# Load order, sine tables, first taps and x's tails in the opening of a two-branch kernel

## The chip, the cores and the metric

The kernel runs on one core of one Trainium2 chip. Its time is the device time of one launch in microseconds (us). Five instruction streams run side by side and wait for each other through semaphores: TensorE (PE: matrix products into PSUM), VectorE (DVE: elementwise), ScalarE (ACT: activations, and copies out of PSUM), GpSimd (POOL: here mostly constants, and DMAs that add), and SyncE (SP: issues DMAs).

## The reference, cut to what matters

Two unrelated branches share the inputs' shape (2048 rows, 576 columns, bf16); their outputs stand side by side.

```
# branch A: dilated local attention, 32 heads of 18, 8 positions at distance 2
qkv = x @ wqkv
logits[s, w] = q[s] . k[s - 2 w] * 18 ** -0.5       # masked where s - 2 w < 0
o = softmax(logits) @ v[s - 2 w];  a = o @ wo
# branch B: a short convolution, a gate, a long convolution, a gate
k_shift[s] = sum over t < 4 of k[s - t] * shift_k[:, t]
kv = k_shift * v
y = causal convolution of kv with ssm_k over 2048 positions, by FFT   # float32
y = y + kv * ssm_D;   b = q * y
out = concat(a, b)
```

## The kernel before, in words

Branch A projects x by wqkv. PE needs x transposed (columns on partitions): 4 blocks of 128 columns and a tail of 64. The first half of x (rows 0 to 1023) comes in two quarters by plain DMA and is transposed on PE (`transpose_x`, `tail_x`, L450 and L455), then copied from PSUM by ACT and, for two blocks of the first quarter, DVE (L510, L511, L521, L460). The second half comes by transposing DMAs (`turn_x`, L236); its tail comes by plain DMA (L235) and is transposed on PE in `transpose_tail` (L473, evicted by ACT L475). `x5(jj)` holds the tails of half jj: its lower 64 partitions those of one quarter, its upper 64 those of the other.

`project_first(jp, ct0)` (L483, L485, evicted at L487) makes q for 256 columns of quarter jp; four calls do the first half of q. `project` (L363 for the four blocks, L374 for the tails, evicted at L397) appends the rest as small pieces of work, "units", for column tiles ct and halves jj. So the jj = 1 units are the first users of the second half of x.

Branch B works on four blocks of 512 rows. `taps(i)` is DVE work: products of k with the four tap weights `skb` (L560), sums (L564), a product with v (L580). The weights are spread over the partitions by PE and ACT (`spread_taps`, L496, L499). k is held as seven rows per partition, 0 to 6; output row c of tap j reads row j + c, so the newest tap (3) reads rows 3 to 6 and tap 2 rows 2 to 5. Block 0's k is loaded in two pieces, rows 3 to 6 and then rows 0 to 2; partition 0 has a memset on POOL and a small POOL DMA of its own (L190, L191). `mirror` folds a finished block on PE (L589) and ACT (L592). The convolution is done by products with tables of sines: TK for the filter, TX for kv, TI (TX transposed on PE in `table_i`, L438, evicted at L442) for the way back. A table is made of an int32 product and offset on DVE (L421, twice), an AND that takes it modulo the period (L422), and a Sin on ACT (L423). The transforms of the filter are L610, L611 and L670, those of kv L766 and L768.

Each engine's order is written out by hand. Work for PE and ACT is held in `units`; `until()` takes as many from its front, at a given place in the DVE work, as the next number in `PLACES` says. `AT` says where the folds go into `units`, `FKS` and `FXS` how the two kinds of transforms and v's projections are interleaved. DVE work stands in program order: four blocks of taps, logits (L822), softmax, weighted sums (L947), spectral products (L1098). SP issues its DMAs in program order: x's first quarter, wqkv's q part, x's second quarter, k's block 0, the k part, v's block 0, k's block 1, x's second half, v's block 1, and so on. After eight DMAs a semaphore is used again, and the ninth waits for the first to land. POOL makes its constants (`identn` to `identn2`, L247 to L298) in program order, with `zero_pads` (L410, L412) behind them. There are two kinds of PSUM buffers, A and B, two of each, that are handed out in turn.

Of the kernel before, what the change touches and what calls it, by code (L numbers as in the profile page):

```python
# [12 lines left out]
ALU = mybir.AluOpType  # L13
FP32 = mybir.dt.float32
BF16 = mybir.dt.bfloat16
I32 = mybir.dt.int32
PSUM = bass.MemoryType.PSUM

PLACES = (
    15, 4, 11, 2, 1, 0, 3, 4, 6, 4, 13, 4, 4, 0, 4, 3, 4, 2, 1, 3, 4, 3, 5, 5, 0, 7, 2, 2, 2, 1, 2, 2, 2, 2, 3,  # L20
    1, 0, 3, 2, 0, 8, 3, 0, 1, 12, 1, 1, 0,
)

FKS = (
    3, 1, 0, 0, 0, 0, 0, 0, 0, 0, 0, 0, 0, 0, 0, 0, 0, 0, 1, 0, 0, 0, 0, 2, 0, 0, 2, 0, 0, 0,
)
FXS = (
    7, 2, 0, 12, 13, 2, 0, 0, 4,
)
# [5 lines left out]
AT = (  # L35
    2, 10, 17,
)
# [8 lines left out]
def kernel(  # L46
# [89 lines left out]
    def load_w(eng, comp, to=None):  # L136
        low, high = (to[:, 0:4, :], to[:, 4, :]) if to is not None else \
            (view(xw, w_at(0, comp), [[D, 4], [1, D]]), wq(4, comp, 0, D))
        eng.dma_start(low, A_wqkv[0:512, comp * D:(comp + 1) * D].rearrange("(kb p) a -> p kb a", p=128))
        for r in range(2):  # L140
            eng.dma_start(high[64 * r:64 * r + 64, :], A_wqkv[512:576, comp * D:(comp + 1) * D])

# [40 lines left out]
    def load_k(i):  # L183
# [5 lines left out]
        if i == 0:  # L189
            nc.gpsimd.memset(kj[0:1, 0:3, :], 0.0)  # L190
            nc.gpsimd.dma_start(kj[0:1, 3:7, :], kf[0:4, :].unsqueeze(0))  # L191
            low = [(1, 49), (49, 64)]
        for a, b in ((3, 7), (0, 3)) if i == 0 else ((0, 7),):
            for p0, p1 in low:
                eng.dma_start(kj[2 * p0:2 * p1:2, a:b], bass.AP(
                    tensor=kf.tensor, offset=kf.offset + (r0 + 4 * p0 - 3 + a) * D,
                    ap=[[4 * D, p1 - p0], [D, b - a], [1, D]]))
# [31 lines left out]
    load_w(nc.sync, 0)  # L229
    load_x(1)  # L230

    def turn_x(h):

        r0 = 1024 + 512 * h
        nc.sync.dma_start(xnat[:, 2 + h, :, 512:576], xf[r0:r0 + 512, 512:576].rearrange("(sb p) c -> p sb c", p=128))  # L235
        nc.sync.dma_start_transpose(view(xw, 6 * HB + 512 * h, [[1024, 4], [1, 512]]), xf[r0:r0 + 512, 0:512])  # L236

# [59 lines left out]
    nc.gpsimd.tensor_scalar(ident2[:], ident[:], 2.0, None, op0=ALU.mult)  # L297
    nc.gpsimd.tensor_scalar(identn2[:], ident[:], -2.0, None, op0=ALU.mult)  # L298

    qk = main.tile([128, 4 * S + 1024 + 4 * KW + KWH], BF16, name="qk")  # L300
# [114 lines left out]
    zero_pads(1)  # L415
    nc.vector.tensor_copy(rp[:], rp_i[:])
    nc.vector.tensor_scalar(rp[64:128, 4:8], rp[64:128, 4:8], -510.0, None, op0=ALU.add)

    def table(n_i, T, vec, cols, period, offs):
        for n in range(2):  # L420
            nc.vector.tensor_scalar(n_i[:, n, :], vec, rp[:, cols[n]:cols[n] + 1], offs[n], op0=ALU.mult, op1=ALU.add)  # L421
        nc.vector.tensor_single_scalar(n_i, n_i, period - 1, ALU.bitwise_and)  # L422
        return lambda: nc.scalar.activation(T, n_i, ACT.Sin, bias=pib[:], scale=-2.0 * np.pi / period)  # L423

# [39 lines left out]

    def early(f, us):
        f()
        clk["P"] += us

    def transpose_tail(jj):
        pt = pp.tile([128, 512], FP32, name="ps_x", tag="B")  # L470
        for jp in range(2):
            for sb in range(4):
                nc.tensor.matmul(pt[64 * jp:64 * jp + 64, 128 * sb:128 * sb + 128], xnat[:, 2 * jj + jp, sb, 512:576],  # L473
                                 ident[:], start=True, stop=True, tile_position=(0, 64 * jp))
        nc.scalar.activation(x5(jj), pt[:], ACT.Copy)  # L475

    def project_first(jp, ct0):
# [25 lines left out]
    spread_taps(0)  # L503
    sines = [table_k(0), table_k(1)]
    pts = [pair_x() for _ in range(2)]
# [7 lines left out]
    spread_taps(256)  # L513
    sines += [table_x(0), table_x(1)]
    project_first(0, 0)
    pts = [pair_x() for _ in range(2)]
    for n in range(2):
# [4 lines left out]
    copy_tail(1, pts[0])  # L522
    project_first(0, 2)
    sines[2]()
    for n in range(2):
        project_first(1, 2 * n)
        sines[3 - 3 * n]()
    for jj in range(2):
        if jj:
            project(0, jj)  # L530
        project(1, jj)
        if jj == 0:
            units.append((0.43, partial(early, partial(transpose_tail, 1), 0.43), "x"))
    project(0, 2)
    project(1, 2)

    def with_sine(f, n):
        f()
        sines[n]()
        if n == 1:  # L540
            nc.gpsimd.memset(TK[0:1, 0, 1, :], 0.5)
            for gi, sg in enumerate((1, -1, -1, 1)):
                nc.gpsimd.memset(TK[0:1, 0, 0, 128 * gi:128 * gi + 128], sg * 0.5)

    for n in range(2):
        units.insert(4 + 4 * n, (0.85, partial(early, partial(table_i, n), 0.85), "x"))
    for n, u in zip((1,), (1,)):
        units[n] = units[n][:1] + (partial(with_sine, units[n][1], u),) + units[n][2:]
# [5 lines left out]
    def taps(i):  # L554
# [12 lines left out]
        if i == 0:  # L567
            mult(view(kv, 0, [[4 * D, 1], [D, 4], [1, D]]), 3, 1)
            mult(view(tB, 0, [[4 * D, 1], [D, 4], [1, D]]), 2, 1)
            add(pair[0])  # L570
# [733 lines left out]
```

## Time and profile before

| what | value |
|---|---|
| runs (three) | 213.08, 213.27, 213.81 us; median 213.27 |
| profiled execution, span from first to last instruction | 211.5 us |
| the profiled execution's own time | not listed; its span is 1.8 us below the median |
| busy: PE, DVE, ACT, POOL | 200.9, 197.3, 151.0, 69.3 us |
| granted TensorE clock, mean | 0.998 |
| DMA, moved over the span | 36.12 MB, mean 171 GB/s |

In the timeline a row has start, length, engine, line, operation, result and operands, and in brackets the idle time of that engine before it and what ended it; rows in a run are merged (x8). In the groups by line a row has the count, the busy total and the mean of one in ns. In the chain of work that ended last a row has start, length and what ran; it gives a PE instruction only the time until the next could go, so its lengths are a bit shorter than those of the timeline. "DMA to landing" counts from the issue. L numbers are lines of the kernel before.

### The profile page before, as it was taken

Reading aid. Unit: us, or ns where it says so; the run is one execution under the profiler, and the core shown is the slowest. Engines: PE = TensorE matmul, PEld = TensorE weight load, DVE = VectorE, ACT = ScalarE, POOL = GpSimd, SP = SyncE. Lnnn points to the kernel's source line nnn. Section 1 sums busy time; section 2 is a strip of 40 time slices with the busy share of each in tenths; the row PEclk is TensorE's granted clock in tenths of the full one; section 3 lists DMA queues with packets and bytes.
Section 4 is the critical chain, followed back from the end, with each engine's and each line's share of the span. In section 5 each row is a group of like instructions: output and inputs, shape, how many; then the busy total and the mean of one; then the engine's idle time right before and its main releaser. Section 6 shows DMA issues by size and latency. Waiting matters only on the chain.

```text
span 211.5 us, 5096 instructions
## 1 busy us (share of the span) xinstructions
PE 200.9 (95%) x2122; PEld 112.5 (53%) x2122; DVE 197.3 (93%) x150; ACT 151.0 (71%) x218; POOL 69.3 (33%) x104
## 2 busy tenths in 40 slices
PE   7999899999879999999999999999999999999891
PEld 2543344445545556563345566765567667676560
DVE  7989999999978999979979999999999999899982
ACT  3799766967797989984378688864487896765640
POOL 8999991023391367220090000004240000202000
PEclk9999999999999999999999999999999999999999
DMA  6999999999092636998999896589993105453034
GB/s 204 297 317 239 248 323 322 183 238 286 8 135 33 87 56 105 187 159 187 226 222 228 141 232 154 103 211 249 209 278 107 60 3 160 123 167 115 3 106 117
DMA packets 34084, 36.12 MB, mean 171 GB/s; under 512 B 17459, under 2 KB 28847, under 8 KB 34062
## 3 DMA queue, kind: packets, MB, share of 16 engines
q1 hardware_dynamic: 26380, 23.11, 43.8%
q0 software_dynamic: 5216, 10.19, 24.8%
q10 hardware_dynamic: 2466, 2.51, 3.6%
q8 instruction: 16, 0.26, 0.5%
q14 instruction: 6, 0.05, 0.1%
HBM read 13.11 MB, written 4.72 MB: 84 GB/s over the span
## 4 chain that ended last, share of the span: by engine, by line
PE 78%; ACT 10%; issue 3%; SPq 2%; DVE 2%; DMA 2%; DVEq 0%; ACTq 0%
PE ps_proj L363 13%; PE ps_z L1126 9%; PE ps_wo L1020 8%; PE ps_acc L964 7%; PE ps_inv L1158 7%; PE ps_fx L766 7%; PE ps_log L837 4%; PE ps_proj L483 4%; PE ps_fk L610 3%; ACT Ks L670 3%; PE ps_proj L374 2%; DMA Ks<-Ks 2%; SPq L212 2%; PE ps_rev L650 1%; PE ps_sk L496 1%
## 5 line engine op out<-in xcount | busy, mean ns | idle before, releaser
L363 PE MATMUL ps_proj<-xw 128*128 128x512 bf16 x160 | 37.5, 380 | 0.5 <-ACT qk L397 0.5
L822 DVE TENSOR_TENSOR av<-qk 128x4096 bf16<-128x4096 bf16 (+1 forms) x16 | 31.5, 2017 | 1.9 <-ACT xw L592 1.9
L363 PEld LDWEIGHTS <-xw 128*128 128x128 bf16 x160 | 14.4, 98 | 20.1 <-issue 4.8
L1139 ACT ACTIVATE av<-ps_z 128x768 bf16<-128x768 f32 x23 | 17.5, 811 | 5.6 <-PE ps_z L1126 5.6
L768 ACT ACTIVATE xw<-ps_fx 128x576 bf16<-128x576 f32 x32 | 18.8, 673 | 2.4 <-PE ps_fx L766 2.4
L397 ACT ACTIVATE qk<-ps_proj 128x1024 bf16<-128x1024 f32 x14 | 14.3, 1025 | 8.3 <-PE ps_proj L374 4.7
L670 ACT ACTIVATE Ks<-ps_fk 128x576 bf16<-128x576 f32 x32 | 19.0, 688 | 1.1 <-PE ps_fk L611 1.0
L1098 DVE TENSOR_TENSOR qk<-xw,Ks 128x2304 bf16<-128x2304 bf16 x14 | 18.6, 1355 | 1.0 <-PE ps_z L1126 0.7
L560 DVE TENSOR_TENSOR tB<-kj,skb 128x4608 bf16<-128x4608 bf16 (+1 forms) x8 | 19.3, 2416 | 0.1
L766 PE MATMUL ps_fx<-xw,TB 128*128 128x288 bf16 x128 | 17.9, 286 | 0.8 <-ACT xw L592 0.7
L1020 PE MATMUL ps_wo<-qk 128*128 128x288 bf16 x128 | 17.9, 287 | 0.0
L610 PE MATMUL ps_fk<-Ks,TB 128*128 128x384 bf16 x62 | 16.4, 326 | 1.2 <-ACT Ks L670 0.9
L1158 PE MATMUL ps_inv<-av,TI 128*128 128x288 bf16 (+1 forms) x112 | 15.6, 292 | 0.6 <-ACT av L1139 0.6
L766 PEld LDWEIGHTS <-TB 128*128 128x128 bf16 x128 | 12.0, 98 | 6.7 <-issue 3.5
L964 PE MATMUL ps_acc<-av,ident 64*64 64x512 bf16 x160 | 15.3, 379 | 0.0
L611 PE MATMUL ps_fk<-Ks,TB 128*128 128x192 bf16 x62 | 15.2, 246 | 0.0
L1087 POOL DMA_DIRECT2D TB<-in_B_q_dram x4 | 3.0, 738 | 36.7 <-DVE v L1098 23.5
L397 ACT ACTIVATE v<-ps_proj 128x1024 bf16<-128x1024 f32 x9 | 9.3, 1043 | 7.8 <-PE ps_proj L363 4.3
L1020 PEld LDWEIGHTS <-qk 128*128 128x128 bf16 x128 | 11.5, 98 | 6.2 <-issue 3.6
L968 ACT ACTIVATE qk<-ps_acc 128x1024 bf16<-128x1024 f32 x8 | 8.2, 1025 | 8.3 <-PE ps_acc L964 8.3
L947 DVE TENSOR_TENSOR av<-Ks,v 128x4096 bf16<-128x4096 bf16 x6 | 13.6, 2285 | 0.1
L1158 PEld LDWEIGHTS <-TI 128*128 128x128 bf16 x112 | 10.5, 98 | 5.6 <-issue 2.7
(194 smaller groups left out, 465.7 us busy)
## 6 DMA issues: line engine op xcount, KB each, us to landing
Ks<-Ks POOLq DMA_DIRECT2D x7, 576.0 KB, 8.3
TB<-av SPq DMA_DIRECT2D x12, 256.0 KB, 4.9
kj<-in_B_k_dram SPq DMA_DIRECT2D x6, 504.0 KB, 6.1
vt<-in_B_v_dram SPq DMA_DIRECT2D x8, 288.0 KB, 5.0
Ks<-av SPq DMA_DIRECT2D x8, 256.0 KB, 6.0
out_dram<-qk ACTq DMA_DIRECT2D x5, 288.0 KB, 3.2
Ks<-in_A_x_dram SPq DMA_DIRECT2D x2, 576.0 KB, 5.2
xw<-in_A_wqkv_dram SPq DMA_DIRECT2D x2, 576.0 KB, 6.0
```

The costliest lines, as they stand in the source:

```text
L363: nc.tensor.matmul(ps[:, jp, :], wq(kb, comp, 128 * ct, 128), xT(kb, 1024 * jj + 512 * jp, 512), **se)
L397: nc.scalar.activation(view(t, o + pad + 1024 * jj, [[512, 2], [1, 512]]), ps[:], ACT.Copy)
L560: dve(2304 * n, lambda: nc.vector.tensor_tensor(to, view(kj, row * D, [[D, n], [D, 4], [1, D]]), view(skb, row * D, [[D, n], [0, 4], [1, D ...
L610: nc.tensor.matmul(o[:, 0:2], w, rhs[:, 0:2], start=start, stop=stop)
L670: nc.scalar.activation(view(Ks, k_at(m, cs ^ (m & 1)) + 96 * gi, [[768, 3], [384, 2], [1, 96]]), acc3(ps), ACT.Copy, scale=(PSG, MSG)[cs][ ...
L766: nc.tensor.matmul(ps[:, pm, 0:HD], TX[:, 2 * pm + c, 128 * gi:128 * gi + 128], kv[:, 2 * c + pm, HD * h:HD * h + HD], start=(c == 0), sto ...
L768: nc.scalar.activation(view(xw, HB * XG[i] + 96 * gi + 1152 * h, [[HB, 2], [384, 3], [1, 96]]), view(ps, 0, [[512, 2], [96, 3], [1, 96]]), ...
L822: return P, at, step, dve(1024 * nj, lambda: nc.vector.tensor_tensor(view(P, at, [[step, 4], [256, nj], [1, 256]]), view(t, o + 256 * hh, ...
L964: nc.tensor.matmul(acc[64 * o:64 * o + 64, h, :], ident[64 * h:64 * h + 64, 64 * h:64 * h + 64], view(P, 256 * u, [[2048, 2], [1, 256]])[6 ...
L1020: nc.tensor.matmul(ps[:, r, 0:HD], oT(hh, j + 2 * r, t)[:, o:o + 128], wo[:, t // 2, t % 2, HD * h:HD * h + HD], start=(t == 0 and h == 0) ...
L1126: nc.tensor.matmul(view(acc[r], 512 * h, [[192, 2], [96, 2], [1, 96]])[o:o + 64], w[64 * h:64 * h + 64, 64 * h:64 * h + 64], pr[64 * h:64 ...
L1158: nc.tensor.matmul(ps[:, c, 0:n], TI[:, sl, pm, 128 * c:128 * c + 128], Yall[:, j % 2, pm, sl, c0:c0 + n], start=(pm == 0 and sl == 0), st ...
```

## The change

It has five parts and new schedule numbers.

- Loads: block 0's k rows 3 to 6 are issued ahead of x's second quarter, in two DMAs that include partition 0 (the POOL DMA L191 goes); rows 0 to 2 follow it. The 64 tail rows of each weight load go to both halves of the partitions by one DMA in place of two.
- Tables: the factors are scaled so that the period is 65536. The low 16 bits of the int32 product, read as a signed 16-bit number, are the phase, so the AND goes. TX is made first, ahead of TK; its sines run on ACT right after the third spread of the weights, and TI is made from it around the transposes of x's second quarter. TK's sines are attached to the second and fourth unit. TK's second half is multiplied out on DVE inside the taps of block 0.
- Taps of block 0: the product of row 2 is split into outputs 1 to 3, which need rows 3 to 5 alone, and output 0.
- Tails of x's second half: the first transposing DMA takes five blocks (the fifth holds the 64 tail columns, and 64 columns more that are overwritten); for the second quarter of that half a transposing DMA of the last 128 columns goes to `xend`, and a POOL DMA moves its upper 64 partitions into `x5(1)`. `transpose_tail` goes.
- Order: two `project_first` calls stand ahead of the second quarter's transposes, and the schedule numbers differ.

```
 PLACES = (
-    15, 4, 11, 2, 1, 0, 3, 4, 6, 4, 13, 4, 4, 0, 4, 3, 4, 2, 1, 3, 4, 3, 5, 5, 0, 7, 2, 2, 2, 1, 2, 2, 2, 2, 3,
-    1, 0, 3, 2, 0, 8, 3, 0, 1, 12, 1, 1, 0,
+    5, 15, 9, 3, 0, 1, 3, 4, 6, 8, 10, 3, 4, 0, 4, 3, 3, 3, 1, 4, 3, 3, 5, 5, 0, 7, 2, 2, 2, 1, 2, 2, 2, 2, 3,
+    1, 0, 3, 2, 1, 14, 3, 0, 1, 18, 1, 1, 0,
...
-    3, 1, 0, 0, 0, 0, 0, 0, 0, 0, 0, 0, 0, 0, 0, 0, 0, 0, 1, 0, 0, 0, 0, 2, 0, 0, 2, 0, 0, 0,
+    3, 0, 0, 1, 0, 0, 0, 0, 0, 0, 0, 2, 0, 0, 0, 0, 1, 0, 0, 0, 0, 0, 0, 0, 0, 0, 2, 0, 0, 0,
...
-    7, 2, 0, 12, 13, 2, 0, 0, 4,
+    7, 15, 3, 5, 5, 2, 0, 0, 4,
...
 AT = (
-    2, 10, 17,
+    0, 7, 20,
...
-        for r in range(2):
-            eng.dma_start(high[64 * r:64 * r + 64, :], A_wqkv[512:576, comp * D:(comp + 1) * D])
+        eng.dma_start(high, A_wqkv[512:576, comp * D:(comp + 1) * D].unsqueeze(0).to_broadcast([2, 64, D]))
...
             nc.gpsimd.memset(kj[0:1, 0:3, :], 0.0)
-            nc.gpsimd.dma_start(kj[0:1, 3:7, :], kf[0:4, :].unsqueeze(0))
-            low = [(1, 49), (49, 64)]
         for a, b in ((3, 7), (0, 3)) if i == 0 else ((0, 7),):
-            for p0, p1 in low:
+            if (i, a) == (0, 0):
+                load_x(1)
+            for p0, p1 in low if i or a else ((1, 49), (49, 64)):
...
     load_w(nc.sync, 0)
-    load_x(1)
...
-        r0 = 1024 + 512 * h
-        nc.sync.dma_start(xnat[:, 2 + h, :, 512:576], xf[r0:r0 + 512, 512:576].rearrange("(sb p) c -> p sb c", p=128))
-        nc.sync.dma_start_transpose(view(xw, 6 * HB + 512 * h, [[1024, 4], [1, 512]]), xf[r0:r0 + 512, 0:512])
+        def turn(to, n, c0):
+            nc.sync.dma_start_transpose(to, bass.AP(tensor=xf.tensor, offset=xf.offset + (1024 + 512 * h) * D + c0,
+                                                    ap=[[D, 512], [1, 128 * n]]))
+        if h == 0:
+            turn(view(xw, 6 * HB, [[1024, 5], [1, 512]]), 5, 0)
+            return
+        turn(view(xw, 6 * HB + 512, [[1024, 4], [1, 512]]), 4, 0)
+        turn(xend, 1, D - 128)
+    xend = view(Ks, 7 * HB, [[1, 512]])
...
     nc.gpsimd.tensor_scalar(identn2[:], ident[:], -2.0, None, op0=ALU.mult)
+    nc.gpsimd.dma_start(x5(1)[64:128], xend[64:128])
...
-    nc.vector.tensor_copy(rp[:], rp_i[:])
-    nc.vector.tensor_scalar(rp[64:128, 4:8], rp[64:128, 4:8], -510.0, None, op0=ALU.add)
+    nc.vector.tensor_scalar(rp[:, 0:4], rp_i[:, 0:4], 32.0, None, op0=ALU.mult)
+    nc.vector.tensor_scalar(rp[0:64, 4:8], rp_i[0:64, 4:8], 16.0, None, op0=ALU.mult)
+    nc.vector.tensor_scalar(rp[64:128, 4:8], rp_i[64:128, 4:8], -510.0, 16.0, op0=ALU.add, op1=ALU.mult)
...
-            nc.vector.tensor_scalar(n_i[:, n, :], vec, rp[:, cols[n]:cols[n] + 1], offs[n], op0=ALU.mult, op1=ALU.add)
-        nc.vector.tensor_single_scalar(n_i, n_i, period - 1, ALU.bitwise_and)
-        return lambda: nc.scalar.activation(T, n_i, ACT.Sin, bias=pib[:], scale=-2.0 * np.pi / period)
+            nc.vector.tensor_scalar(n_i[:, n, :], vec, rp[:, cols[n]:cols[n] + 1], offs[n] * (65536 // period),
+                                    op0=ALU.mult, op1=ALU.add)
+        low = n_i.rearrange("p n f -> p (n f)").bitcast(I16).rearrange("p (n f w) -> p n f w", n=2, w=2)[:, :, :, 0]
+        return lambda: nc.scalar.activation(T, low, ACT.Sin, scale=2.0 * np.pi / 65536)
...
-    sines = [table_k(0), table_k(1)]
+    sines = [table_x(0), table_x(1)]
...
     spread_taps(256)
-    sines += [table_x(0), table_x(1)]
+    sines.append(table_k(0))
+    sines[0]()
+    sines[1]()
     project_first(0, 0)
+    project_first(0, 2)
+    table_i(0)
...
     copy_tail(1, pts[0])
-    project_first(0, 2)
-    sines[2]()
+    table_i(1)
     for n in range(2):
         project_first(1, 2 * n)
-        sines[3 - 3 * n]()
...
-        if jj == 0:
-            units.append((0.43, partial(early, partial(transpose_tail, 1), 0.43), "x"))
...
-    for n in range(2):
-        units.insert(4 + 4 * n, (0.85, partial(early, partial(table_i, n), 0.85), "x"))
-    for n, u in zip((1,), (1,)):
+    for n, u in zip((1, 3), (2, 3)):
...
-            mult(view(tB, 0, [[4 * D, 1], [D, 4], [1, D]]), 2, 1)
+            for c, n in ((1, 3), (0, 1)):
+                dve(n * D, lambda: nc.vector.tensor_tensor(
+                    pair[0][:, c:c + n], kj[:, 2 + c:2 + c + n], skb[:, 2:3, :].to_broadcast([128, n, D]), ALU.mult))
+                if c:
+                    sines.append(table_k(1))
```

More of the change, by code (lines that the diff above doesn't have):

```diff
@@ L16 @@
 I32 = mybir.dt.int32
+I16 = mybir.dt.int16
 PSUM = bass.MemoryType.PSUM
 PLACES = (
-    15, 4, 11, 2, 1, 0, 3, 4, 6, 4, 13, 4, 4, 0, 4, 3, 4, 2, 1, 3, 4, 3, 5, 5, 0, 7, 2, 2, 2, 1, 2, 2, 2, 2, 3,
-    1, 0, 3, 2, 0, 8, 3, 0, 1, 12, 1, 1, 0,
+    5, 15, 9, 3, 0, 1, 3, 4, 6, 8, 10, 3, 4, 0, 4, 3, 3, 3, 1, 4, 3, 3, 5, 5, 0, 7, 2, 2, 2, 1, 2, 2, 2, 2, 3,
+    1, 0, 3, 2, 1, 14, 3, 0, 1, 18, 1, 1, 0,
 )
 FKS = (
-    3, 1, 0, 0, 0, 0, 0, 0, 0, 0, 0, 0, 0, 0, 0, 0, 0, 0, 1, 0, 0, 0, 0, 2, 0, 0, 2, 0, 0, 0,
+    3, 0, 0, 1, 0, 0, 0, 0, 0, 0, 0, 2, 0, 0, 0, 0, 1, 0, 0, 0, 0, 0, 0, 0, 0, 0, 2, 0, 0, 0,
 )
 FXS = (
-    7, 2, 0, 12, 13, 2, 0, 0, 4,
+    7, 15, 3, 5, 5, 2, 0, 0, 4,
 )
@@ L463, in pair_x @@
         return pp.tile([128, 2, 1024], BF16, name="ps_x", tag="B")
[L465 to L475, printed above, removed]
     def project_first(jp, ct0):
@@ L539, in with_sine @@
         sines[n]()
-        if n == 1:
+        if n == 3:
             nc.gpsimd.memset(TK[0:1, 0, 1, :], 0.5)
```

## The prediction

> **What bounds the kernel now.** I read the page's first part, then the busy times by stage, the chain of work that ended last, the waits of VectorE (DVE), and last the instructions in order of time up to 64 us. Engine totals, from the page:
>
> ```profile
> span 211.5 us, 5096 instructions
> PE 200.9 (95%) x2122; PEld 112.5 (53%) x2122; DVE 197.3 (93%) x150; ACT 151.0 (71%) x218; POOL 69.3 (33%) x104
> ```
>
> Two engines are nearly full, so the order in which they wait for each other decides. By stage (columns: stretch, length, then busy us and count for PE, PEld, DVE, ACT, POOL, the granted clock, DMA share, GB/s):
>
> ```profile
> 24.00:53.00 29.00, 29.00 (x202) 12.48 (x203) 28.52 (x17) 20.48 (x28) 11.22 (x23) 1.00 1.02 270
> 53.00:64.00 11.00, 8.85 (x85) 5.56 (x84) 9.18 (x9) 9.48 (x16) 6.96 (x9) 1.00 0.52 74
> 64.00:107.00 43.00, 42.08 (x380) 22.81 (x376) 40.58 (x25) 33.08 (x52) 14.56 (x14) 1.00 0.73 131
> 107.00:180.00 73.00, 72.90 (x910) 44.94 (x902) 71.85 (x49) 53.68 (x79) 11.05 (x15) 1.00 0.71 169
> ```
>
> From 24 to 53 us PE does not stop at all. From 53 to 64 it loses 2.15 us, DVE 1.82 us, and ACT (9.48 of 11) is the fullest. After that PE is full again. Two of DVE's later waits, and rows of the timeline at 64 us with the longest one:
>
> ```profile
> DVE av L882 <- ACT av L879: 1.3, 1, 1.3
> DVE av L947 <- PE ps_log L837: 1.1, 1, 1.1
> ```
>
> ```profile
> 63.34 1.05 PE L837 MATMUL ps_log<-av,E 128*32 128x512 bf16 x16
> 64.06 3.43 DVE L822 TENSOR_TENSOR av<-qk 128x4096 bf16<-128x4096 bf16 x2 [1.85 <-ACT xw L592]
> ```
>
> DVE had three logit products ready and stood 1.85 us, until 64.06, for a buffer that PE's first L837 group (from 63.34) empties. So at 64 us DVE is early and PE late, and the later waits too are for PE or ACT. What the first 53 us do to PE therefore passes to the end; what they do to DVE does not, as long as the DVE wait stays above zero.
>
> **The change: VectorE.** Rows that price it, of the groups, the timeline, and L179's landing times:
>
> ```profile
> L421 DVE TENSOR_SCALAR Ks<-Ks,rp 128x512 int32<-128x512 int32 x8 | 3.6, 494 | 0.0
> L422 DVE TENSOR_SCALAR Ks<-Ks 128x1024 int32<-128x1024 int32 x4 | 2.8, 708 | 0.1
> 11.96 1.36 DVE L560 TENSOR_TENSOR xw<-kj,skb 128x2304 bf16<-128x2304 bf16 x1 [0.82 <-DMA kj<-in_B_k_dram]
> 16.02 2.56 DVE L560 TENSOR_TENSOR tB<-kj,skb 128x4608 bf16<-128x4608 bf16 x1
> 26.75 2.56 DVE L560 TENSOR_TENSOR tB<-kj,skb 128x4608 bf16<-128x4608 bf16 x1
> 3.12 0.59 SPq L179 DMA_DIRECT2D Ks<-in_A_x_dram  x1
> DMA to landing us min/median/max: 4.1/5.2/6.3
> 8.28 1.02 ACT L499 ACTIVATE skb<-ps_sk 128x1024 bf16<-128x1024 f32 x1
> ```
>
> Four ANDs go (2.8 us). Block 0's first product now starts at 11.96, after waiting for k. Moved ahead of x's second quarter, k's first block (equally large) takes that quarter's place: issue 3.12 plus the longer of the two landings of that line, 6.3, is 9.4. The tap weights are out at 8.28 + 1.02 = 9.3. So the product starts near 9.4, 2.56 us earlier. Behind it now stand the last table's two products (3.6 / 8 = 0.45 each, 0.9) and a split product: from 1.36 for 2304 elements and 2.56 for 4608 an instruction's fixed part is 0.16. The three small instructions that replace the cast and the subtraction add one such 0.16 before 9.4, in time that is free. DVE ends block 0 ahead by 2.56 - 0.9 - 0.16 = 1.5 us. This buys nothing: the 1.85 us wait becomes 3.3. If k landed no sooner than now, DVE would be 1.06 late, still inside the 1.85.
>
> **TensorE and ScalarE up to 24 us.** The sines of TX now run before the first projection's eviction, and both inverse tables (L438) surround the transposes of x's second quarter.
>
> ```profile
> 7.79 1.91 PE L483 MATMUL ps_proj<-xw 128*128 128x512 bf16 x8
> 10.17 1.07 PE L450 MATMUL ps_x<-ident,Ks 128*128 128x128 bf16 x16
> 11.51 1.90 PE L483 MATMUL ps_proj<-xw 128*128 128x512 bf16 x8
> 11.62 1.94 ACT L521 ACTIVATE xw<-ps_x 128x1024 bf16<-128x1024 bf16 x2 [0.32 <-PE ps_x L455]
> 23.84 1.08 ACT L442 ACTIVATE TI<-ps_ti 128x512 bf16<-128x512 f32 x2
> 24.00 1.89 PE L363 MATMUL ps_proj<-xw 128*128 128x512 bf16 x8 [0.55 <-ACT qk L397]
> ```
>
> ```profile
> 20.88 1.02 ACT qk L397
> 21.90 1.04 ACT TB L423
> 27.39 0.57 PE ps_ti L438 x16
> 28.93 0.35 PE ps_x L473 x8
> 29.28 1.83 PE ps_proj L363 x8
> ```
>
> The second fence is of the chain of work that ended last. One early projection takes PE 10.17 - 7.79 = 2.38, x's transposes 11.51 - 10.17 = 1.34. PE afterwards: projection to 10.17, second to 12.55, first table to 13.12, transposes to 14.46, second table to 15.03. ACT: free at 9.3, two sines 2 x 1.04 to 11.38, eviction (1.02) to 12.40, so the table's PSUM is free in time; the second eviction can start at 12.6 and ends at 13.6; table eviction 1.08 to 14.7; copies of x 0.97 each, to 15.65 and 16.6. The third projection needs the first copy for its first two matmuls (1.83 / 4 = 0.46) and the second for the next: PE stands 0.6 and then 0.5, together 1.1 us. Gone are the 0.55 wait at 24.00 and the tail transposes (0.35). Sum on PE: 1.1 - 0.55 - 0.35 = **+0.2 us**. From both sides: if ACT's sines did not delay the copies, -0.9; if PE also stood for the table's PSUM as at 24.00, +0.75. I take +0.2, since every term but the waits is a row. x's second quarter lands 2 us later (behind 590 KB more), at 11.4, and is wanted at 13.1: hidden, 1.7 us of cover.
>
> **x's tails by DMA.** PE loses its eight transposes and ACT one copy. SP loses the two tail loads, and one of each pair of weight loads and of k's split loads, about 0.59 us of issue each (the row at 3.12), and gains a fifth block in the first transposing DMA and a third one. POOL loses its k DMA and gains one that moves the second half's tail, and PE's jj = 1 tails wait for it. Behind it on POOL stand memsets for k's pads and TK, and the filter's copies, which wait for their data until 42.2. Behind the transposes on SP stand block 1's v and block 2's k; if these come late, DVE loses some of a lead that buys nothing. Rows of source lines and of the timeline, and a fold from the chain:
>
> ```profile
> L236 SPq DMA_TRANSPOSE xw<-in_A_x_dram x2: 2422/3606/4789, 14.9 to 20.9; - x2
> DMA to landing us min/median/max: 4.8/6.6/8.3
> 3.84 0.87 POOL L191 DMA_DIRECT2D kj<-in_B_k_dram  x1
> 11.61 0.20 POOL L277 TENSOR_SCALAR_AFFINE_SELECT E<-ones 128x32 bf16<-128x32 bf16 x1
> 16.13 2.52 POOL L279 TENSOR_SCALAR_AFFINE_SELECT E<-E 64x32 bf16<-64x32 bf16 x1
> 29.66 1.42 POOL L298 TENSOR_SCALAR identn<-ident 128x128 bf16<-128x128 bf16 x1
> L726 POOL DMA_DIRECT2D Ks<-Ks x3: 538/543/632, 42.2 to 47.7; - x3
> DMA to landing us min/median/max: 2.5/3.4/4.3
> 35.53 0.61 PE ps_fold L589 x8
> ```
>
> When PE wants it: the first jj = 1 matmul is at 29.28 now; plus 0.2, plus a fold (0.61) that the new AT puts ahead of it, 30.1; its tails come 1.83 later, **31.9**. When it lands: the DMA is queued on POOL behind L298, which ends at 31.08 now. A POOL operation that takes 0.20 at 11.61 takes 2.52 beside DVE's product of 16.02 and ends when that ends: one passes per DVE product, eleven between 11.96 and 31.08. In the new order POOL starts 0.87 earlier, and DVE, free of the ANDs, stands from about 7.9 to 9.4, where six selects pass; I estimate 13 left at 9.4, give or take three. The thirteenth DVE instruction from there is block 1's second double product, which ends at 26.75 + 2.56 = 29.3 now and at 27.8 then. The transposes: SP reaches the first about 2 us sooner, near 13; 5/4 of 4.79 brings it to 19, the second (2.4 to 4.8) to 21.4 to 23.8, and the last lands 4.8 later, 26.2 to 28.6. So the POOL DMA starts at about 28 and lands 3.4 later, 31.4: 0.5 us before PE wants it. I count 0. The ends are 0 (26.2 + 2.5 is long before) and 4.3: three more POOL operations pass with three more DVE products of 1.36, to 31.9, and land 4.3 later, at 36.2.
>
> [...]
>
> **Reordered fillers.** Two transforms of x (0.5 us of PE each) and two of the filter (0.49 each) move ahead of the fifth logit group.
>
> ```profile
> 78.52 1.02 ACT L842 ACTIVATE av<-ps_log 128x1024 bf16<-128x1024 f32 x1 [0.18 <-PE ps_log L837]
> 82.87 0.20 DVE L865 TENSOR_TENSOR av<-av,maskb 32x128 bf16<-32x128 bf16 x1
> ```
>
> That eviction ends 2 us later, at 81.5, and its reader starts at 82.87: hidden, 1.3 us of cover. A transform moved behind the L837 group at 106.47 can cut the last DVE wait of 1.1 by 0.5; PE is full there, so I count 0 and keep -0.5 for the range.
>
> **Sum.** +0.2 on a span of 211.5, 211.7. The span is 1.8 below the median of the runs, 213.27, and I carry that over: **213.5 us**.
>
> **Rivals.** *The tail lands late*: POOL passes fewer selects than I estimate and PE stands at its first jj = 1 tails. It decides from a landing after 31.9. One or two products more (1.36 each, less the 0.5) cost 0.9 or 2.2, on average 1.5: 213.5 + 1.5 = 215.0. For it: only 0.5 us of cover on a chain of thirteen steps; against: POOL's head start. *DVE's lead arrives*: the folds are done sooner, and PE's and ACT's idle time at 53 to 64 us (2.15 and 1.52) shrinks by the lead, 213.27 - 1.5 = 211.8. For it: DVE is 93% busy and has hardly a wait from 64 to 180; against: at 53 to 64 it waits for PE, and the last fold's operand was already there. It decides if the 1.85 us wait shrinks rather than grows. *No change from loading k first*: the start at 9.4 fails because ACT's weights or k come late; by the 1.06 above that ends in 213.5 too.
>
> **How the numbers follow.** About 0.3% (0.64 us) is what a measurement of this kernel can tell from no change. Likeliest case 0.44, its own range 212.6 to 214.2 (-0.9 and +0.75 about zero): same 0.35, slower 0.06, faster 0.03. Late tail 0.30: slower. Lead arrives 0.26: faster 0.25, same 0.01. Together faster 0.28, same 0.36, slower 0.36. The range, 211.6 to 215.8, takes in both rivals' values; beyond it, with some 0.15, lie the last 2 us of the late tail and reorderings that add to the lead.
>
> **What would show it.** Right: block 0's first product near 9.4; the first L822 after the negations waiting over 3 us; PE standing about 1.1 us around 15 to 17; no PE wait on a POOL DMA near 32; first L837 near 63.5. Wrong: PE standing at L374 near 32, a first L837 before 62.9, or the third projection starting without a wait.

## The result, and the profile after

The changed kernel takes **219.34 us** in the median of six runs (216.76 to 220.75), the kernel before 213.32 beside it (212.92 to 214.28): the ratio is **1.025, 95% interval 1.020 to 1.029**. The forecast was 213.5 with a range of 211.6 to 215.8, so it missed, by 5.8 us. The six times of the changed kernel lie 4.0 us apart, those of before 1.4. That scatter is the kernel's own, as will be seen; the ratios and intervals leave out executions more than 1.5% above the fastest of a kernel, so I give the extremes too.

The execution shown took 220.37 us, 1.7 above its span. The page's first part, and the busy times by stage (columns as in the prediction):

```profile
span 218.7 us, 5070 instructions
PE 203.1 (93%) x2114; PEld 112.6 (51%) x2114; DVE 195.2 (89%) x148; ACT 150.1 (69%) x217; POOL 55.6 (25%) x104
```

```profile
24.00:53.00 29.00, 25.78 (x125) 9.82 (x124) 26.54 (x15) 16.66 (x21) 3.62 (x11) 0.88 1.04 262
53.00:64.00 11.00, 10.32 (x94) 5.80 (x93) 10.90 (x9) 8.09 (x12) 2.30 (x4) 1.00 0.34 98
64.00:107.00 43.00, 41.03 (x376) 23.00 (x374) 36.23 (x25) 36.20 (x59) 17.96 (x18) 1.00 0.71 115
107.00:180.00 73.00, 72.46 (x870) 42.90 (x868) 70.91 (x48) 51.86 (x75) 12.28 (x16) 1.00 0.75 176
```

The span is 7.2 us longer. From 24 to 53 us, where PE did not stop before, it now stands 3.2 us, and its granted clock is 0.88. In the later stages the differences of PE's busy time cancel (10.32 in place of 8.85, but 41.03 in place of 42.08 and 72.46 in place of 72.90). So the place to look is one stage. The timeline of PE there, with one row of the opening ahead of it:

```profile
10.00 0.60 PE L484 MATMUL ps_proj<-xw 64*128 64x512 bf16 x2 [0.94 <-DMA xw<-in_A_wqkv_dram]
...
31.94 0.39 PE L383 MATMUL ps_proj<-xw 64*128 64x512 bf16 x1
35.55 1.01 PE L383 MATMUL ps_proj<-xw 64*128 64x512 bf16 x3 [3.22 <-DMA xw<-Ks]
36.49 3.59 PE L372 MATMUL ps_proj<-xw 128*128 128x512 bf16 x8
40.02 1.17 PE L590 MATMUL ps_fold<-xw,fold 128*64 128x288 bf16 x8
```

PE asks for the tails of x's second half at 31.94, as forecast (31.9), and then stands 3.22 us for the POOL DMA that moves them (L307 of the kernel after). What follows it runs at half speed: eight matmuls take 3.59 in place of 1.90, a fold 1.17 in place of 0.68. The same stretch by clock:

```profile
32.20:35.50 3.30, 0.13 (x1) 0.00 (x0) 2.27 (x2) 0.00 (x0) 0.00 (x0) 0.93 0.96 330
35.50:41.00 5.50, 5.45 (x19) 1.68 (x18) 4.38 (x3) 1.90 (x2) 0.00 (x0) 0.50 1.17 373
```

The clock is 0.50 behind the standstill, and not only to the end of this stretch: read in narrower stretches it falls at 35.07 and is back at 41.90. PE is at work for 6.35 us of that, so 3.2 us of work are lost. Wait and half clock make 6.4 of the 7.2 us. The rest is spread over other waits.

Why the tail came so late is in the chain of waits (start, length, what):

```profile
2.65 8.24 DMA kj<-in_B_k_dram
10.90 1.78 SPq L204
14.76 8.98 SPq L234
23.79 2.54 SPq L234
26.37 2.98 DMA Ks<-in_A_x_dram
29.99 5.51 DMA xw<-Ks
```

Read from the bottom: POOL's DMA is issued at 29.99 and takes 5.51; it waited for the third transposing DMA, which SP issues at 26.37, behind the two long ones of 8.98 and 2.54. And SP reached the first of those only at 14.76 (12.90 in experiment 1 below), because of DMAs of the opening that landed late: it stands 1.8 us, until 9.97, for one of wqkv's loads, and the next long step in the chain starts at 10.90, when block 0's k has landed. At the top of the chain stands block 0's k, issued at 2.65 and landed 8.24 us later. In the kernel before the same loads land in 5 to 7 us. Landing times of block 0's k (two lines of code, issues up to 9.5 us), first of the kernel before, then of the changed one:

```profile
L195 SPq DMA_DIRECT2D kj<-in_B_k_dram x4: 576/716/943, 3.8 to 6.9; - x4
DMA to landing us min/median/max: 5.5/6.2/6.7
L198 SPq DMA_DIRECT2D kj<-in_B_k_dram x2: 670/704/739, 5.4 to 7.8; - x2
DMA to landing us min/median/max: 5.1/5.1/5.1
```

```profile
L195 SPq DMA_DIRECT2D kj<-in_B_k_dram x3: 590/919/1154, 2.6 to 5.8; - x3
DMA to landing us min/median/max: 8.2/8.7/9.1
L198 SPq DMA_DIRECT2D kj<-in_B_k_dram x2: 663/677/691, 3.3 to 6.8; - x2
DMA to landing us min/median/max: 7.6/8.0/8.4
```

What stands behind the q part's weight tail lands about 3 us later than it did, and the row at 10.00 above shows the tail itself landing late: PE waits for it (it was issued at 1.88). DVE sees the same: block 0's first product does not start at 9.4.

```profile
11.82 1.36 DVE L557 TENSOR_TENSOR xw<-kj,skb 128x2304 bf16<-128x2304 bf16 x1 [4.31 <-DMA kj<-in_B_k_dram]
...
36.55 2.56 DVE L557 TENSOR_TENSOR tB<-kj,skb 128x4608 bf16<-128x4608 bf16 x1 [2.05 <-DMA kj<-in_B_k_dram]
...
70.79 3.43 DVE L823 TENSOR_TENSOR av<-qk 128x4096 bf16<-128x4096 bf16 x2 [5.41 <-ACT xw L593]
```

DVE waits 4.31 us for k at the start and 2.05 for block 2's, and still stands 5.41 us before the fourth logit product (1.85 before). DVE is late and is not the bound: PE is later still.

### The profile page after: what moved, and what is told of

The parts are those of the page before. It is cut to its first block, busy times and chain, and to the rows that moved or that the text cites. A ratio compares the mean times of both kernels' runs of the same rounds, so it can differ in the third digit from the quotient of the medians.

```text
span 218.7 us, 5070 instructions
## 1 busy us (share of the span) xinstructions
PE 203.1 (93%) x2114; PEld 112.6 (51%) x2114; DVE 195.2 (89%) x148; ACT 150.1 (69%) x217; POOL 55.6 (25%) x104
## 4 chain that ended last, share of the span: by engine, by line
PE 63%; DMA 11%; SPq 9%; ACT 7%; DVE 4%; issue 4%; DVEq 0%; ACTq 0%; POOLq 0%
PE ps_proj L372 12%; PE ps_z L1127 9%; PE ps_inv L1159 7%; PE ps_wo L1021 5%; SPq L234 5%; PE ps_fx L767 5%; PE ps_acc L965 4%; PE ps_fk L611 4%; DMA kj<-in_B_k_dram 4%; PE ps_log L838 4%; DMA TB<-av 3%; DMA xw<-Ks 3%; PE ps_proj L376 2%; PE ps_proj L383 2%; DVE av L948 2%
## 5 line engine op out<-in xcount | busy, mean ns | idle before, releaser
L372 PE MATMUL ps_proj<-xw 128*128 128x512 bf16 x160 | 39.2, 395 | 0.0
L372 PEld LDWEIGHTS <-xw 128*128 128x128 bf16 x160 | 15.0, 100 | 21.5 <-issue 6.9
L557 DVE TENSOR_TENSOR tB<-kj,skb 128x4608 bf16<-128x4608 bf16 x7 | 17.9, 2556 | 2.2 <-DMA kj<-in_B_k_dram 2.0
L1162 ACT ACTIVATE v<-ps_inv 128x576 bf16<-128x576 f32 (+1 forms) x14 | 9.5, 675 | 5.1 <-PE ps_inv L1159 5.1
```

What stands on the lines that cost most here:

```text
L372: nc.tensor.matmul(ps[:, jp, :], wq(kb, comp, 128 * ct, 128), xT(kb, 1024 * jj + 512 * jp, 512), **se)
```

## The experiments

**Theory A**: the weight tail as one DMA (`to_broadcast([2, 64, D])`, both halves of the partitions) holds up the loads behind it, and x's tail is only where this shows. **Theory B**: x's tail by DMA is late by itself. **Theory C**: loading k first makes the loads late. **Theory D**: half of the loss is the clock, which falls because PE stands. Each diff is against the changed kernel unless it says otherwise; line numbers in an experiment's rows are of its own kernel, a few off those of the changed one.

**1. Two weight tail DMAs again.**

```
-        eng.dma_start(high, A_wqkv[512:576, comp * D:(comp + 1) * D].unsqueeze(0).to_broadcast([2, 64, D]))
+        for r in range(2):
+            eng.dma_start(high[64 * r:64 * r + 64, :], A_wqkv[512:576, comp * D:(comp + 1) * D])
```

> The changed kernel with only the weight tails undone: two DMAs of 64 rows for each weight part, as before. Theory A (the one DMA that writes both halves holds up everything queued behind it): block 0's k lands 5 to 7 us after its issue in place of 8.2 to 9.1, the first product starts at 9.4 to 10 in place of 11.82, the second half's transposing DMAs are issued 2 us or more sooner, the tail lands before 33 in place of 35.5, PE stands under 1 us for it, the clock stays at 1.00, and the time is 212.5 to 214.5. Theory B (x's tail by DMA is late by itself, by a transposing DMA of five blocks, a third one and a DMA of POOL): PE still stands more than 2.5 us near 32 to 36, and the time is 217 or more.

215.28 us (214.22 to 219.00, five runs), ratio 1.007 (1.004 to 1.010). Timeline rows of DVE and PE, and the landing of block 0's k:

```profile
9.88 1.36 DVE L558 TENSOR_TENSOR xw<-kj,skb 128x2304 bf16<-128x2304 bf16 x1 [2.12 <-ACT skb L499]
```

```profile
33.16 0.59 PE L384 MATMUL ps_proj<-xw 64*128 64x512 bf16 x3 [0.86 <-DMA xw<-Ks]
```

```profile
L196 SPq DMA_DIRECT2D kj<-in_B_k_dram x3: 574/616/944, 3.1 to 5.8; - x3
DMA to landing us min/median/max: 5.0/5.4/5.8
```

The loads land in 5.0 to 5.8 again, DVE starts at 9.88 and waits for ACT's weights rather than for k, and PE stands 0.86 in place of 3.22. By the medians four of the 6 us come back with one line. But not all: the tail still lands at 33.1, 1.2 after PE asked, and two of the five runs took 218 and 219. Theory A carries the larger part, and something of B is left.

**2. The kernel before with the one weight tail DMA alone** (the reverse edit on the kernel before).

> The kernel before with only the weight tails changed: one DMA that writes both halves. Theory A: x's second quarter, k's blocks and v land 8 to 9 us after their issue in place of 5 to 6.5; block 0's first product starts at 13.5 to 14.5 in place of 11.96; the transposing DMAs end 2 us or more later, PE stands 1 to 3 us for them near 29, and the time is 215 to 218. Theory B and theory C (k ahead of x's second quarter makes the loads late): landings as before, 213.3 give or take 0.7.

216.12 us (215.15 to 217.20), ratio 1.014 (1.009 to 1.019). Block 0's first product starts at 13.81, and no other part of the change is in it: this one line makes the kernel before slower by 3 us. PE loses it in the opening, rather than near 29 us as I had put it:

```profile
12.16 1.07 PE L449 MATMUL ps_x<-ident,Ks 128*128 128x128 bf16 x16 [1.31 <-DMA Ks<-in_A_x_dram]
...
13.65 3.38 PE L482 MATMUL ps_proj<-xw 128*128 128x512 bf16 x8
```

PE stands 1.31 us for x's second quarter, which lets it go only 9.5 us after its issue, and the projection behind it takes 3.38 in place of 1.90: here too the clock is at half, from 13.27 to 16.69.

**3. x's second quarter ahead of k again.**

```
             if (i, a) == (0, 0):
-                load_x(1)
...
     load_w(nc.sync, 0)
+    load_x(1)
```

> The changed kernel with only the order of the loads undone: x's second quarter ahead of block 0's k. Theory C (k first makes the loads late): the tail lands by 32, no wait of PE for it, 213 to 215. Theory A: the loads stay at 8 to 9 us, block 0's first product moves later by the length of one quarter, to 13 to 15, PE still stands 2.5 us or more for the tail, and the time is 218 to 221.

219.93 us (218.47 to 221.62). The first product moves to 13.41 and PE still stands 2.63 us for the tail. Theory C falls: the order of the loads is not what made them late.

**4. PE kept at work through the wait.**

```
             body(ps, ct, jj, jp, first)
+            if (comp, ct, jj, jp) == (0, 0, 1, 1):
+                for n in range(14):
+                    nc.tensor.matmul(ps[:, 1, :], zw[:], xT(0, 0, 512), start=False, stop=False)
```

`zw` is a tile of zeros, so the matmuls add nothing to the projection.

> The changed kernel with 14 matmuls of 512 columns by a zero weight (about 3.2 us at full clock, they add zeros to the projection that waits) put where PE stands for the tail. The stall is the same, but PE works through it. Theory D (the half clock from 35.5 to 41 us is a consequence of the standing, and costs 2.9 us beside the 3.2 of the wait): the granted clock is 1.00 from 32 to 41, the projection behind the tail takes 1.83 in place of 3.52, and the time is 2.5 to 3.2 below that of the changed kernel, 216 to 217, as in its one execution at a mean clock of 0.999 (216.76). If the clock is independent of the standing, 219 to 220.

217.25 us (216.58 to 217.53), 2.1 below the changed kernel, and the scatter is gone from 4.0 to 1.0 us. The same two stretches as above:

```profile
32.20:35.50 3.30, 3.30 (x18) 1.35 (x17) 2.28 (x2) 0.00 (x0) 0.00 (x0) 1.00 1.01 347
35.50:41.00 5.50, 5.50 (x34) 2.03 (x33) 4.57 (x3) 3.42 (x5) 0.00 (x0) 1.00 1.11 366
```

The tail is as late as before (PE goes on at 35.23), but the clock stays at 1.00. So the half clock is a consequence of PE standing, and by the medians of this pair of kernels it costs about 2 us; theory D holds, a little below its size. The size differs between executions. In the order of their times, from 216.76 to 220.75 us, the changed kernel's six had mean clocks of 0.999, 0.991, 0.986, 0.985, 0.978 and 0.977, and the one at 0.999 took what this experiment takes; the execution shown above is one of the two with most half clock.

The half clock lasts 6.83 us in the changed kernel and 3.41 in experiments 2, 3, 8 and 9. The length of the standstill does not decide by itself whether it comes: the clock fell after one of 1.31 us in experiment 2, and after one of 2.63 in experiment 3, but not after 2.65 in experiment 6 below. The traces show what goes with it: in each of these executions every change of the clock lies a whole multiple of 3.413 us from the others (in the changed kernel, from 4.35, where the full clock starts, to the fall at 35.07 are nine). PE's work in the stretches of that length in which it stood, with the clock in them (columns: stretch, length, PE's busy us and count, clock, DMA share, GB/s), first of the changed kernel, then of experiments 2 and 3, then the two of experiment 6:

```profile
31.66:35.07 3.41, 0.67 (x3) 1.00 0.91 298
```

```profile
9.86:13.27 3.41, 1.71 (x20) 1.00 0.97 267
```

```profile
31.47:34.88 3.41, 1.07 (x5) 1.00 0.88 300
```

```profile
29.49:32.91 3.42, 2.20 (x10) 1.00 0.89 292
32.91:36.32 3.41, 1.97 (x10) 1.00 1.04 376
```

Behind the first three the clock fell; the standstill of experiment 6 lies across two stretches, both had about 2 us of work, and it did not fall. The stretches in experiments 8 and 9 fit (0.55 and 0.84, a fall). In all the profiles of this case a fall stands behind every such stretch with 1.71 us of work or less, and behind none with 1.91 or more. So in these runs it is where the standstill lies that counts and not its length alone.

**5. x's tails on PE again, the one weight tail DMA kept, and both undone.** `turn_x` loads the tails plainly and takes four blocks as before, `transpose_tail` runs with the first unit of the second half, and POOL's DMA goes. The second kernel has edit 1 as well.

> The changed kernel with only x's tails undone: they are loaded plainly and transposed on PE ahead of the first projection of the second half, as before; the weight tails stay one DMA each. Theory A (the weight tails make all loads late, x's tail is only the place where it shows): the loads stay late (first product of block 0 near 11.8, block 2's k waited for by DVE), PE does not stand 3 us near 32 and the clock stays at 1.00 there; 214 to 216.5. Theory B (the tail by DMA is the whole cost): 212.5 to 214.

> The changed kernel with both undone: x's tails on PE and two DMAs for each weight tail. What is left is the order of the loads, the sine tables, block 0's taps and the schedule. By the prediction's working (DVE's lead buys nothing, PE gains or loses some tenths before 24 us): block 0's first product at 9.4 to 10, no wait of PE above 1.1 us, the wait of DVE for the logits near 64 us over 2 us, 213.3 give or take 0.7. If DVE's lead reaches the end: 211.5 to 212.3. If both theories miss a cost: 214.5 or more.

With the weight tails kept: 214.86 us (214.59 to 215.33), ratio 1.009 (1.006 to 1.011). With both undone: **213.29 us** (212.86 to 214.28, ten runs), ratio 1.001 (1.000 to 1.003). So the late loads alone cost 1.6 us, x's tail by DMA alone (experiment 1 against this) 1 to 2 us in three executions and 5 in two, and both together 6: late loads cost most where something with no cover hangs on them. The kernel with both undone is what the prediction was about apart from its two misjudged steps. Its rows on DVE:

```profile
9.68 1.36 DVE L566 TENSOR_TENSOR xw<-kj,skb 128x2304 bf16<-128x2304 bf16 x1 [1.91 <-ACT skb L500]
...
64.46 2.29 DVE L832 TENSOR_TENSOR av<-qk 128x4096 bf16<-128x4096 bf16 x1 [3.12 <-ACT xw L602]
```

The first product starts at 9.68 (9.4 was forecast), and the wait near 64 us is 3.12 (3.3): DVE's lead turned into a longer wait there.

**6. Only the k part's tail in one DMA** (the q part's in two).

> The changed kernel with the q part's tail in two DMAs again and the k part's tail in one. Theory A says that the one DMA holds up what is queued behind it and nothing ahead of it: block 0's k and x's second quarter land 5 to 6.5 us after their issue and the first product starts at 9.9, as with both tails in two; block 0's v and block 1's k land 7.5 to 9.5 after theirs, as in the changed kernel; PE stands 1.5 to 3.5 us for the tail near 32; 215.5 to 219. If the lateness came from the number of DMAs or from semaphores used again and not from the form of this one, all loads would land alike, early or late.

216.78 us (215.39 to 218.63). Block 0's k and x's second quarter, ahead of that DMA, land in 5.0 to 5.9 and 6.3, and DVE's first product starts at 9.27. Block 0's v, right behind it:

```profile
L208 SPq DMA_DIRECT2D vt<-in_B_v_dram x1: 569/569/569, 8.9 to 8.9; - x1
DMA to landing us min/median/max: 8.9/8.9/8.9
```

8.9 (5.0 before, 5.7 in experiment 1); a DMA of block 1's k takes 8.9 too, which says less, since one of them took 8.0 in experiment 1. What is ahead of the DMA is on time and v right behind it is late, in one and the same run.

**7. Half of the columns in one DMA.**

```
+        for r in range(2):
+            eng.dma_start(high[64 * r:64 * r + 64, 288:D], A_wqkv[512:576, comp * D + 288:(comp + 1) * D])
+        eng.dma_start(high[:, 0:288], A_wqkv[512:576, comp * D:comp * D + 288].unsqueeze(0).to_broadcast([2, 64, 288]))
```

> The changed kernel with the left half of each weight tail's columns loaded by one DMA for both halves of the partitions, and the right half by two DMAs. [...] The time follows the landing of x's tail, 214 to 218.

215.39 us (214.79 to 215.84). If the delay goes with the bytes, block 0's k lands half way between the 5.0 to 5.8 us of two DMAs and the 8.2 to 9.1 of one, at 6.6 to 7.5; if it is a fixed price of the form, at 8.2 to 9.1 again:

```profile
L197 SPq DMA_DIRECT2D kj<-in_B_k_dram x3: 521/572/900, 3.8 to 6.8; - x3
DMA to landing us min/median/max: 5.3/6.1/6.9
```

5.3 to 6.9, where one DMA for all columns gave 8.2 to 9.1 and two gave 5.0 to 5.8. So the delay is less with fewer bytes and is no fixed price of the form. It is less than in proportion: 0.3 to 1.1 us later than with two in place of half of 3.2. Why the first half costs less was not settled.

**8. The q part's one DMA on ACT's queue.**

```
+        if comp == 0:
+            nc.scalar.dma_start(high, A_wqkv[512:576, comp * D:(comp + 1) * D].unsqueeze(0).to_broadcast([2, 64, D]))
```

with the k part's tail in two on SP's queue.

> The changed kernel with the q part's tail still one DMA, but issued by ACT on its own queue, and the k part's tail in two DMAs on SP's. It tells how the one DMA holds up the others. If what is behind it in the same queue waits for it: with the DMA on another queue block 0's k lands 5 to 6.5 us after its issue, the first product starts at 9.3 to 10, and only the q tail itself is late. If it is the shared DMA engines that are busy with it: block 0's k lands at 7 to 9 as in the changed kernel (8.2), and the first product starts at 10.5 to 12. The time is 213 to 218 in both, by x's tail, and decides nothing.

218.88 us (two runs); here the time is lost in the opening, and the tail matmuls at 36.55 wait for nothing. The second DMA of block 0's k, and PE's wait for the q tail:

```profile
L202 SPq DMA_DIRECT2D kj<-in_B_k_dram x1: 667/667/667, 2.5 to 2.5; - x1
DMA to landing us min/median/max: 7.6/7.6/7.6
```

```profile
12.94 0.60 PE L488 MATMUL ps_proj<-xw 64*128 64x512 bf16 x2 [3.00 <-DMA xw<-in_A_wqkv_dram]
```

k still needs 7.6 us (5.1 without such a DMA) although nothing of the kind is ahead of it on SP's queue, x's second quarter 10.0; the first product starts at 10.22, between the two expectations, since k was issued 0.8 sooner. And the one DMA itself, issued at 1.47, lets PE go only at 12.94, with the clock at half from 13.49 to 16.90. So the lateness is no matter of the order within one queue: a DMA on ACT's queue made loads on SP's 2.5 and 3.7 us later. How this DMA ran shows in the trace's records of single packets, since it is the only large one on ACT's queue in the opening: its 128 packets run from 5.32 to 12.21 us, at most two at a time (more than two for 0.07 us in all), while some 15 of SP's queue are under way at once. Its 144 KB (128 rows of 1152 bytes) so took 6.9 us, 21 GB/s by these times, and with both tails in one DMA on SP's queue block 0's k, behind the first, came 3.2 us later. What limits it to two at a time was not shown: its outermost dimension is two, and it also reads its rows twice, and no load with only one of the two was run.

**9. The tail turned sooner**: edit 1, and the one-block transposing DMA issued ahead of the four-block one of that quarter.

```
-        turn(view(xw, 6 * HB + 512, [[1024, 4], [1, 512]]), 4, 0)
         turn(xend, 1, D - 128)
+        turn(view(xw, 6 * HB + 512, [[1024, 4], [1, 512]]), 4, 0)
```

> The kernel with two weight tail DMAs, and with the transposing DMA of the last quarter's tail issued ahead of the four-block one of that quarter. In the run with two weight tails POOL was free at 24.67 us and waited until 27.08 for this transpose, and PE stood 0.86 us for POOL's DMA (landed 33.1, asked for at 31.9). If the place in SP's queue is what makes it late: POOL issues at 24.7 to 25, the tail lands at 30 to 31, PE does not stand for it, the clock holds in every execution, and the time is 212.7 to 213.9, without the executions of 218 and 219 of the run with two weight tails. If POOL or the landing limits: PE stands as there, 214.2 to 219.

Ten runs in two groups: five from 212.57 to 213.35, one at 215.38, four from 217.57 to 218.45. The execution shown is of the slower group. POOL there, and then in experiment 1:

```profile
25.34 2.62 POOL L306 TENSOR_SCALAR identn<-ident 128x128 bf16<-128x128 bf16 x1
27.92 0.74 POOL L308 DMA_DIRECT2D xw<-Ks  x1
```

```profile
22.08 2.59 POOL L306 TENSOR_SCALAR identn<-ident 128x128 bf16<-128x128 bf16 x1
...
27.08 0.74 POOL L308 DMA_DIRECT2D xw<-Ks  x1 [2.41 <-DMA Ks<-in_A_x_dram]
```

The transpose was ready at 24.4, but POOL reached its DMA only at 27.92, from the last constant, without a wait. In experiment 1 the same constant was done at 24.67. Most of the constants pass one for each product of DVE (this last one took 2.62 and 2.59 us beside products of 2.56 and 2.64), and DVE's first product came at 9.07 here and 9.88 there: three constants fewer had passed by then, and POOL ended 3.25 us later. Then the DMA took 6.5 us (issued 0.74), PE stood 3.01, and the clock fell. In this execution POOL's program decides, and the outcome hangs on tenths of a microsecond at 9 us. (PE's first sixteen transposes took 1.07 us here and 1.91 in experiment 1, so ACT's weights, for which DVE waits, came sooner.) That this is what parts the two groups is inferred: no execution of the faster one was profiled. In the changed kernel itself POOL had been done by 17.5, since late loads kept DVE off.

**10. The move by SP**: edit 9, and the move into the upper partitions issued by SP behind block 1's v in place of by POOL.

```
-    nc.gpsimd.dma_start(x5(1)[64:128], xend[64:128])
...
     load_v(1)
+    nc.sync.dma_start(x5(1)[64:128], xend[64:128])
```

> The kernel with two weight tail DMAs and the tail turned sooner, with the move into the upper partitions issued by SP behind block 1's v in place of by POOL. In the profiled execution with the tail turned sooner POOL came to its DMA at 27.92, held back by one constant for each product of DVE, without waiting for the transpose, and PE stood 3.01 us. If POOL's place behind DVE is what is left: SP issues at 25 to 26.5, the tail lands by 31, PE does not stand for it in any execution, and all executions lie at 212.5 to 213.5, as the better ones of the kernel before this did, none at 217 to 218.5. If the landing after the issue is as long as POOL's 5 to 6 us: 31 to 32.5, PE stands up to 0.7, 213 to 214. DVE's block 2 may wait 0.7 longer for its k, which costs nothing.

**212.98 us** (212.44 to 213.48, nine runs), ratio 0.999 (0.998 to 1.000). The move is issued at 25.4 and lands in 3.1 us:

```profile
L253 SPq DMA_DIRECT2D xw<-Ks x1: 520/520/520, 25.4 to 25.4; - x1
DMA to landing us min/median/max: 3.1/3.1/3.1
```

```profile
31.66 0.61 PE L384 MATMUL ps_proj<-xw 64*128 64x512 bf16 x4
```

PE's four tail matmuls run without a wait, and in nine runs the slow group is gone. This is the best version found; it is not measurably faster than the kernel before. With the loads, the move and the clock mended, the whole change is worth nothing.

**11. DVE's lead taken back**: both undone as in 5, and an AND of the low 16 bits behind each table's products.

```
+        nc.vector.tensor_single_scalar(n_i, n_i, 65535, ALU.bitwise_and)
```

> The kernel with both undone (x's tails on PE, two weight tail DMAs), with an AND of the low 16 bits put back behind each table's products, which changes no value: four operations of 0.71 us on DVE, two of them before block 0's k is there. If DVE's lead buys nothing: DVE is 1.4 to 2.8 us later, its wait for the logits near 64 us falls from 3.12 to between 0.3 and 1.7, and the time stays at 213.3 give or take 0.5. If the lead was worth its length: 214.5 to 216.

213.52 us (213.19 to 213.81, ten runs), ratio 1.001 (1.000 to 1.002), the same as without the ANDs. Three of the four ran in time that DVE had free, so DVE was only 0.6 us later, its wait near 64 us fell by 0.4:

```profile
64.49 2.29 DVE L833 TENSOR_TENSOR av<-qk 128x4096 bf16<-128x4096 bf16 x1 [2.69 <-ACT xw L603]
```

That 0.6 us moved nothing. It is a weaker test than I meant it to be.

## Why the prediction was wrong, step by step

- *PE is the bound to 107 us, and DVE's lead buys nothing*: right. In the kernel with both undone DVE ended block 3 1.2 us sooner than before and the time stayed. It holds in one direction only: with the loads late (first kernel of 5) DVE was 1.9 later than before at block 3's last product, more than the wait of 1.85 by 0.1, but PE lost 0.9 near 57 us already, where it waits for ACT (1.56 in place of 0.68). So the wait at 64 us was probably not the first place where a late DVE reaches PE: that operation of ACT starts right after one of DVE (L645) that is 1.9 late, but the trace names no cause for its wait.
- *Block 0's first product at 9.4*: wrong in the changed kernel (11.82), right without the q part's one DMA (9.1 to 9.9, where it waits for ACT's weights and not for k). The step that failed is "issue 3.12 plus the longer of the two landings of that line, 6.3": I took the landing time of the kernel before, although a DMA of a new form stood ahead in the queue.
- *"one of each pair of weight loads ... about 0.59 us of issue each"*: **the first step that failed**. I counted the merged DMA as issue time saved on SP and gave its transfer no price. It cost about 3 us on every load behind it, 3 us on the kernel before, and about 4 of the 6 here.
- *The third projection waits 0.6 and 0.5 for ACT*: 0.67 and 0.32 in most of these kernels. The opening's +0.2 fits: PE asked for the tails at 31.94 where 31.9 was forecast. That it fits so well is luck: in the changed kernel PE also stood 0.94 for the q part's tail, which no term had, and its first sixteen transposes took 1.07 in place of 1.36; over the experiments in which PE then stood for the tail the time is 31.05 to 32.15.
- *The tail, "lands 3.4 later, 31.4: 0.5 us before PE wants it. I count 0"*: **the second step that failed**. With the loads mended POOL's issue came at 27.1 (experiment 1) and 27.9 (experiment 9), the 28 of the forecast, and in experiment 1 the last transpose landed at 26.5, within the 26.2 to 28.6 of the forecast. Both are partly luck: in experiment 1 POOL was free at 24.67 and waited for the transpose, where the forecast had POOL as the later one, and the first transposing DMA held SP for 7.6 us in place of 6.0 while the last landed in 3.1 in place of 4.8. But the landing of POOL's DMA took 6.0 and 6.5 us, not 3.4, beyond the upper end of 4.3 that I took from L726. In the changed kernel both parts failed: issued at 29.99, landed 5.5 later. L307's issue is short (0.74), as L726's were (0.54 to 0.63). The length was in the landing, most of it ahead of the first packet: that ran 3.4 us after the issue in the changed kernel, 3.8 and 4.2 in experiments 1 and 9, and 2.2 after it where SP moved the same bytes, in 3.1 us. What held it back was not tested.
- *The rival "the tail lands late"*: it is what happened, by its place and condition. Its size was wrong (215.0), because I priced the wait as so much time lost and no more. The wait of 3.22 us was followed by half clock for 6.83 us, and such a price stood in no case of the prediction.
- *The range*: the 4.3 us that I had worked out as the tail's end would have reached 217.8; I left its last 2 us outside. Even that end had no term for the late loads.

## What to carry to other kernels

Merging two loads into one saves an issue (0.72 us on SP in place of 1.22 for the q part's tail), but look first at how the merged access runs and at the loads behind it: here at most two of its packets ran at a time (experiment 8), and what stood behind or beside that DMA came 2.5 to 4 us later. Before a step is moved from an engine to a DMA, write down who issues it and what that queue is held by: here POOL's DMA stood behind constants that passed one for each product of VectorE, and POOL reached it only at 27.92 with its data ready at 24.4 (experiment 9). And price a stall of PE like those here, 1.31 to 3.22 us, twice: once for the wait, once for the half clock that followed five of the six listed below, for 3.41 or 6.83 us.

## What the runs showed of the hardware that was not expected

- A 144 KB load that writes 64 rows to both halves of the partitions delayed loads on its own queue by 2.5 to 4 us, and on another by 2.5 to 3.7 (experiment 8); itself it took 8 us, or over 11 when its queue was not SP's, and there it ran at most two packets at a time.
- The move of x's tail within SBUF (64 KB) took 5.2 to 6.7 us to land when POOL issued it, and 3.1 when SP did. Other DMAs of POOL within SBUF landed in 2.5 to 4.3 (L726 in the prediction), so it is not all of them.
- The clock fell to half after standstills of 1.31, 2.63, 3.00, 3.01 and 3.22 us, and did not after one of 2.65. Its changes lay multiples of 3.413 us apart, and it fell behind each stretch of that length with 1.71 us of PE's work or less and behind none with 1.91 or more (experiment 4). The changed kernel's six executions, at mean clocks of 0.977 to 0.999, lie 4.0 us apart.
- The first transposing DMA held SP for 9.0 us with five blocks in the changed kernel and 7.6 in experiment 1. With four blocks it was 4.8 before and 5.8 in the kernel with both undone, but 7.9 in experiment 2 and in the first kernel of 5, where the loads are late. So its length goes with what else is under way as much as with the fifth block.
